# First group's up products of two quarters in float16, with w_in's bounds in two parts

## The chip, the cores and the metric

The kernel runs on one core of a Trainium2 chip. The time is device microseconds of one execution of the program. The engines are TensorE (PE; its weight loads are PEld), VectorE (DVE), ScalarE (ACT), GpSimd (POOL) and SyncE (SP, which issues nearly all DMAs). Each works off its own instruction list in order.

## The reference

Attention over a few memory slots, then a two-layer feed-forward block. Batch 8, 8 heads, 576 positions, head size 64, 32 slots:

```
a      = softmax(phi)                          # over the 32 slots
k_m, v_m = a^T k, a^T v                        # per head: 32 x 64
x      = softmax(q k_m^T / 8) v_m              # 4608 tokens x 512
h      = x w_in                                # 512 -> 2048
out    = max(0.01 h, h) w_out                  # 2048 -> 512
```

q, k, v and phi are float32. w_in and w_out are float64; the kernel reads their words and makes float32 of them itself.

## The kernel before

The kernel never forms x. It folds the attention's values into the weights: for batch b and quarter j of d_ff (512 of 2048 columns), v_m times w_in's quarter is a 256 x 512 matrix, and h is the attention weights times that matrix. Products of float32 accuracy are either float32 matmuls (four passes in the array, two records each in the trace) or three float16 passes: an operand is split into a float16 hi part and a float16 lo part (the rest), and hi x hi, lo x hi and hi x lo are added up. A split needs a power-of-two scale, which comes from a bound on the weights: squares are summed (ScalarE), transposed on TensorE, turned into a power of two on VectorE and spread to all partitions by a matmul.

Tokens are worked off in groups. Group 0 (384 tokens of batch 0) and group 1 (384 more) go by units of 256 of the 2048 columns; from then on groups of 256 tokens take another route, with one up and seven down products per quarter. Before the change, group 0 is wholly in float32, since the bounds of the weights are not known that early; group 1 and all later ones are in float16.

Every instruction's place is written by hand: two strings, OPENING and LATER, list the steps in order, and each engine gets its instructions in the order of that list. Steps that matter here:

- `i<j>.` and `o<j>.`: quarter j of w_in and w_out. `ld0` to `ld2` load three pieces (768, 768, 512 columns) into one of eight staging slots used in turn, so a load waits until the slot's last reader is done; `h`, `y`, `t` make float32 of a piece (h and y on ScalarE, h on VectorE for some pieces, t on VectorE); `b` sums the squares on ScalarE (L429). `k`, `l` and `s`, `m`, `n` make the float16 parts of the weights and of sums of their blocks.
- `ci.1` to `ci.4` and `co.1` to `co.4` (L489 to L512): the bounds of w_in and w_out, all four quarters at once: transpose, roots on VectorE, spreading matmul, factors on VectorE. `e.` (L1301, L1302): the scales of the folded weights of batches 0 and 1.
- `f0<j>.1` (L1242): the folded products of batch 0, quarter j, in float32 into two PSUM banks. `f0<j>.2` (L1614): ScalarE copies them to SBUF as float32.
- `u<u>.P<i>` (L1340): an up product of group 0, unit u (quarter u // 2), half i: two float32 matmuls of 384 columns. `u.V` (L1347): leaky relu on ScalarE. `u.O` (L1411): down products, three float32 matmuls of 512 columns.
- `W<b><j>.p` (L1242), `.h` (L1275, ScalarE), `.l` (L1281, VectorE): the folded weights of batch b, quarter j, and their float16 hi and lo parts for the halves g = 0, 1. For batch 0 these are made from the float32 copy in SBUF, for batch 1 from PSUM. `w1.1` is W10.p.
- `P<m>`, `V`, `C`, `L`, `O` (m = 8 to 15): the same units for group 1, in float16; C and L make hi and lo of the leaky result. `p`, `v`, `s`, `c`, `l`, `d`: the later groups.
- `a<b>.`: attention of batch b. Here: phi, kv, q (loads), A1 to A3, B0 (maximum of phi), B10, B20 (subtract, exp), C10 (slot sums, L794), D1, D2, D3 (their transposes and scale), E1 (scores, L1088), E2 (flips), S (softmax by chunks).
- `z.`: products of ones that keep TensorE busy at the start.

PSUM tiles named pa have three banks that are used in turn; folded products take two of them.

Of the kernel before, what the change touches and what calls it, by code (L numbers as in the profile page):

```python
# [77 lines left out]
C10 V11.1 W03.h0 a2.kv3 o0.l2 V11.0 o1.l0 W03.h1 o1.m2 o1.k1 O8.0 W12.l1 O8.1 O9.0 o2.k0 C11 P13.0
P12.1 L10 o3.s3 W03.l0 O9.1 o1.l2 o1.n2 o1.m3 i1.l1 o1.l1 a2.B20 L11 O10.0 W03.l1 W13.h0 V12.1 o2.l0
P13.1 o2.k2 o2.s0 V13.0 W13.l0 P12.0 a2.kv1 W13.h1 a2.C10 a2.B3 W13.l1 a1.S17 V13.1 C13 a2.C2 o1.n3  # L80
o2.m0 O10.1 V12.0 i1.l2 C12 o2.s1 O11.0 i2.k0 a2.C30 o2.k1 L12 P14.0 a2.C31 L13 o2.n0 P14.1 O11.1
o2.l1 a2.q0 o2.s2 o2.m1 o2.n1 V14.0 a2.C3k a2.C4 a2.D10 a1.S18 i2.l0 P15.0 V14.1 P15.1 a2.D3 a2.Q0
o2.m2 o2.s3 V15.0 o2.l2 a3.phi C14 O12.0 V15.1 p0.0 o2.m3 o3.k0 v0.0 o3.k2 O12.1 i2.k1 p0.1 o3.s0
C15 p0.2 L14 O13.0 i3.k1 o3.s1 v0.2 a2.q1 a3.A1 a2.Q1 v0.1 L15 a2.E1 p1.0 i2.l1 o3.s2 o3.l0 a2.E21
a2.E22 o3.k1 p0.3 o3.m0 O13.1 v0.3 o3.l1 v1.0 o2.n2 a2.E20 p1.1 c0.0 o2.n3 i2.k2 a3.A2 a2.D2 o3.l2
a2.D11 o3.n0 p1.2 v1.2 O14.0 v1.1 s0 a2.E3 a2.D4 o3.m3 p1.3 a3.A4 o3.m2 a2.E23 c0.1 O14.1 a2.D5 v1.3
O15.0 l0.0 p2.1 o3.m1 a2.S01 O15.1 c1.0 a2.S02 v2.1 o3.n1 a2.S03 Z1.0 l0.1 o3.n3 p2.0 Z1.2 a2.D6
v2.0 a3.A3 o3.n2 d0.0 d0.1 p2.2 d0.5 a3.kv s1 l1.0 p2.3 a2.S04 Z1.1 c1.1 d0.6 d1.1 d1.0 a3.B10 v2.3
# [1646 lines left out]
```

## Time and profile before

| | before |
|---|---|
| three runs | 648.1, 645.9, 647.3 us, median 647.3 us |
| profiled execution's own time | 647.43 us |
| its span, first to last instruction | 645.6 us |
| busy: TensorE, VectorE, ScalarE, GpSimd | 630.3, 529.7, 402.9, 14.3 us |
| share of the span | 98%, 82%, 62%, 2% |
| granted clock of TensorE | 1.00 over the span |
| read from HBM, written | 50.59 MB, 9.45 MB |

The time of the execution is 1.8 us longer than the span. A busy share is an average over stages. Rows of the trace give a line of the kernel (L1340 is line 1340), an engine, an operation and its tiles (output <- inputs); a number in brackets at the end is the time that the engine stood idle just before, and what released it. Matmuls are pipelined: a row's length holds the latency of the last one, so the cost of a matmul in a packed stretch is the distance from one start to the next.

### The profile page before, as it was taken

The page shows a single profiled execution, that of the slowest core. Times are in us where ns is not written, and L with a number is a line of the kernel's source. Part 1 is how long each engine was busy: PE and PEld are TensorE (multiplying, and loading weights), DVE is VectorE, ACT ScalarE, POOL GpSimd, SP SyncE. Part 2 cuts the span into 40 slices and gives each one's busy share as a digit, 9 for nine tenths or more (in the row PEclk, how much of TensorE's full clock was granted, in tenths as well). Part 3 has the DMA queues.
Part 4 walks back from the last instruction along what each step waited for, and adds up shares of the span by engine and source line. Part 5 has one row for each costly group of instructions (what it writes and reads, how often), then busy time and mean ns, then how long its engine had stood idle before and what let it go on. Part 6 is the DMA issues. An engine that isn't in the chain of part 4 may idle for free.

```text
span 645.6 us, 17428 instructions
## 1 busy us (share of the span) xinstructions
PE 630.3 (98%) x7437; PEld 496.7 (77%) x7437; DVE 529.7 (82%) x841; ACT 402.9 (62%) x699; POOL 14.3 (2%) x34
## 2 busy tenths in 40 slices
...
GB/s 318 363 372 274 304 46 4 120 106 13 172 99 42 186 50 83 133 71 78 39 188 22 13 2 101 79 144 46 2 92 19 6 29 33 4 29 6 34 17 50
DMA packets 85404, 61.16 MB, mean 95 GB/s; under 512 B 61648, under 2 KB 68560, under 8 KB 85328
## 3 DMA queue, kind: packets, MB, share of 16 engines
...
q8 instruction: 58, 0.95, 0.6%
q10 hardware_dynamic: 576, 0.56, 0.3%
q14 instruction: 18, 0.15, 0.1%
HBM read 50.59 MB, written 9.45 MB: 93 GB/s over the span
## 4 chain that ended last, share of the span: by engine, by line
PE 52%; DVE 6%; SPq 3%; issue 1%; ACT 1%; DMA 0%; DVEq 0%; ACTq 0%
PE po L1521 27%; PE ph L1453 17%; PE ph L1521 4%; SPq L621 3%; PE pa L1242 2%; DVE arena L1498 1%; DVE arena L986 1%; PE pa L794 1%; DVE r1k L656 1%; PE pa L1044 1%; DVE arena L1488 1%; SPq L1394 0%; DMA arena<-in_q_dram 0%; DVE arena L1489 0%; DVE t L1120 0%
## 5 line engine op out<-in xcount | busy, mean ns | idle before, releaser
L1521 PEld LDWEIGHTS <-arena 128*128 128x128 f16 x2520 | 242.0, 98 | 38.2 <-issue 8.5
L1453 PE MATMUL ph<-a,w_mem 128*128 128x256 f16 (+3 forms) x1656 | 157.0, 243 | 1.0 <-ACT wi L1472 0.7
L1521 PE MATMUL po<-wo,arena 128*128 128x256 f16 x1080 | 139.6, 273 | 1.0 <-DVE arena L1498 0.6
L1521 PE MATMUL po<-arena 128*128 128x256 f16 x1080 | 140.0, 273 | 0.0
L1453 PEld LDWEIGHTS <-w_mem 128*128 128x128 f16 x1656 | 128.6, 98 | 14.8 <-issue 4.6
L1474 ACT ACTIVATE wi<-ph,g_scs 128x256 f32<-128x256 f32 x112 | 53.0, 473 | 82.7 <-PE ph L1453 72.9
L1472 ACT ACTIVATE wi<-ph,g_scs 128x256 f32<-128x256 f32 x112 | 52.9, 472 | 66.1 <-PE ph L1453 64.1
L1498 DVE TENSOR_TENSOR arena<-arena 128x1024 f16<-128x1024 f32 (+1 forms) x58 | 69.9, 1205 | 28.2 <-ACT arena L1494 28.2
L1411 PE MATMUL po<-wo,arena 128*128 128x512 f16 (+1 forms) x240 | 77.1, 467 | 0.8 <-DVE wo L424 0.8
L1494 ACT CAST arena<-arena 128x1024 f16<-128x1024 f32 (+1 forms) x58 | 60.2, 1037 | 21.8 <-DVE arena L1490 17.7
L1498 DVE TENSOR_TENSOR arena<-wi,arena 128x768 f16<-128x768 f32 x56 | 52.9, 948 | 6.0 <-ACT arena L1494 5.9
L1521 PE MATMUL ph<-wo,arena 128*128 128x256 f16 x360 | 48.8, 273 | 0.4 <-DVE arena L1498 0.4
L1494 ACT CAST arena<-wi 128x768 f16<-128x768 f32 x56 | 46.6, 831 | 3.4 <-PE po L1521 2.9
L1488 DVE TENSOR_TENSOR arena<-wi 128x512 f32<-128x512 f32 x56 | 38.5, 687 | 8.5 <-ACT wi L1472 4.3
L1340 PE MATMUL ph<-a,w_mem 128*128 128x192 f16 (+1 forms) x232 | 38.0, 313 | 0.0
L1411 PEld LDWEIGHTS po<-wo,arena 128*128 128x128 f32 x96 | 17.4, 190 | 20.2 <-issue 18.4
L1281 DVE SCALAR_TENSOR_TENSOR w_mem<-pa,w_mem 128x512 f16<-128x512 f32 x40 | 26.9, 681 | 7.0 <-ACT w_mem L1275 7.0
L1242 PE MATMUL pa<-wi,vT 64*32 64x512 f16 (+1 forms) x704 | 29.5, 420 | 0.7 <-DVE w_mem L1281 0.7
L1275 ACT ACTIVATE w_mem<-pa 128x512 f16<-128x512 f32 x40 | 23.1, 598 | 8.1 <-PE pa L1242 2.9
L1490 DVE TENSOR_TENSOR arena<-wi,arena 128x256 f32<-128x256 f32 x56 | 23.8, 425 | 2.0
L1453 PE MATMUL ph<-a,arena 128*128 128x256 f16 (+3 forms) x216 | 24.9, 237 | 0.5 <-ACT wi L1472 0.5
L1489 DVE TENSOR_TENSOR arena<-wi,arena 128x256 f32<-128x256 f32 x56 | 23.8, 425 | 1.9
...
## 6 DMA issues: line engine op xcount, KB each, us to landing
...
```

What stands on the lines that cost most here:

```text
L1242: nc.tensor.matmul(pf[g][cols, :], lhs, rhs, start=(n == 0), stop=(n == len(passes) - 1), tile_position=(g * D, hh * M),)
L1281: nc.vector.scalar_tensor_tensor(tiles(t[:, 1]), w(g), ws, tiles(t[:, 0]), ALU.mult, ALU.subtract)
L1340: nc.tensor.matmul(ph[:, t0:t0 + n], lhs, rhs, start=(m == 0), stop=(m == len(seq) - 1))
L1411: nc.tensor.matmul(po, lhs, rhs, start=(f == 0 and m == 0), stop=(f == NQ * NF - 1 and m == len(seq) - 1),)
L1453: nc.tensor.matmul(ph[:, t0:t0 + n], lhs, rhs, start=(m == 0), stop=(m == len(seq) - 1))
L1472: nc.scalar.activation(dst, ph, AF.Prelu, scale=g_sc2n[:, j:j + 1], alpha=1.0 / SLOPE)
L1474: nc.scalar.activation(dst, ph, AF.Prelu, scale=g_sc2[:, j:j + 1], alpha=SLOPE)
L1488: nc.vector.tensor_tensor(gt[:, 0:2], two, gf[:, 1:3], ALU.subtract)
L1489: nc.vector.tensor_tensor(gt[:, 2], gf[:, 1], gt[:, 1], ALU.subtract)
L1494: nc.scalar.copy(dst[:, 0], src)
L1498: nc.vector.tensor_tensor(dst[:, 1], src, dst[:, 0], ALU.subtract)
L1521: nc.tensor.matmul(acc, g[:, x, s, u], rhs, start=(h == 0 and j == 0 and u == 0 and m == 0), stop=(j == NQ - 1 and u == 1 and m == 2), ski ...
```

## The change

Group 0's up products of quarters 2 and 3 (units u4 to u7) use the float16 parts W02 and W03, in three passes, where quarters 0 and 1 stay in float32. For that:

- The attention weights of group 0 get float16 parts as well: `a0.H0` (a cast on ScalarE) and `a0.H1` (a subtraction on VectorE), 128 x 768 each.
- f02.2 and f03.2, the float32 copies, are gone; W02's and W03's hi and lo parts are made from the products in PSUM, before the units that use them.
- w_in's bounds go in two parts, quarters 0 to 2 (`ci0.1` to `ci0.4`) and quarter 3 (`ci3.1` to `ci3.4`), each through transpose, roots, matmul and factors. The factors also make batch 0's fold scale and `h_sc`, the scale that the leaky step of u4 to u7 applies. `e.` makes batch 1's alone.
- Some buffers are assigned otherwise (`w_turn`, the place of a sum's temporary, and two buffers of the first later group).
- The order is the same for the first 110 steps, up to u1.P0, and another one behind it, in OPENING and in LATER.

```
@@ OPENING, from the 110th step on
-i1.y0 i1.t0 u0.P1 u1.V0 a0.S11 o0.h0 o0.y0 o0.h1 o1.ld1 i1.h2 i2.ld1 a0.S12 o1.ld2 o0.t0 o0.y1 o0.t1
...
-i2.ld0 o1.y0 u1.O1 u2.V1 o2.h0 a0.S14 a0.D4 u2.V0 i2.ld2 i2.h0 o1.t0 o2.ld1 i2.y0 u3.P0 u3.P1 i2.h2
-o1.t2 i2.t0 a1.phi i2.y2 i2.t2 o2.y0 o2.y1 f02.1 o2.ld2 u2.O0 o2.t0 o2.h1 f02.2 u3.V0 a1.A1 o2.h2
-a1.A2 a1.A3 a0.S15 i1.b o2.t1 a1.kv1 u4.P1 a1.B0 a1.kv0 o2.y2 a1.kv2 u3.O0 u3.V1 a1.kv3 u4.P0 a1.q1
-a1.B10 a0.S16 a1.B20 a1.q0 o0.b o2.t2 u4.V0 o1.b o2.b a1.B3 a1.C10 i3.ld1 a1.Q0 a1.C2 a1.C30 u5.P0
-a1.C31 u2.O1 a1.C4 i3.ld0 a1.Q1 i3.ld2 i3.h1 a1.C3k o3.ld2 a1.D11 i2.b a1.D5 a1.D10 a1.D2 u3.O1
-a1.D4 i3.y1 u4.V1 i3.t1 a1.D3 a1.E1 u5.V0 i3.y0 i3.h0 i3.y2 i3.t0 u4.O0 i3.h2 o3.y2 i3.t2 a1.E22
-u5.P1 a1.E20 i3.b a1.S01 a1.E21 a1.S02 f03.1 ci.1 u5.O0 a2.phi o3.h2 a1.S11 a0.S17 o3.ld1 o3.t2
-u5.V1 o3.y1 a1.S03 ci.2 a2.kv2 a1.S12 a0.S18 o3.h1 u4.O1 a2.A1 a1.S04 a1.S13 o3.t1 ci.3 f03.2 a2.A2
-ci.4 o3.ld0 e. w1.1 o3.h0 o3.y0 W00.h0 a1.S05 a1.S06 o3.t0 u6.P0 u7.P0 a1.S14 W10.h0 u6.V0 o0.s0
-W00.h1 a2.A4 o3.b u7.V0 u6.O0 W00.l0 o0.s1 W00.l1 co.1 a1.S07 W01.h0 a2.A3 a2.B10 co.2 u7.P1 W10.h1
-u6.P1 a2.kv0 co.3 a1.S08 i0.k1
+o0.h1 i1.y0 o0.h0 o0.y0 o0.y1 i1.t0 u1.V0 u1.P1 o1.ld1 o0.t0 u1.V1 o0.t1 i1.h1 a0.D2 i1.h2 i2.ld1
...
+o1.t2 i2.t0 a1.phi o2.h0 i2.t2 i2.b o2.t0 o2.ld2 u1.O1 u3.P1 u2.O0 u3.V0 ci0.1 a1.A1 a0.H0 u3.V1
+a1.A2 a1.kv1 o2.y1 ci0.2 o2.y2 u2.P1 a1.A3 a1.kv0 a0.H1 a1.kv2 ci0.3 a1.kv3 ci0.4 o2.h1 a1.B0 f02.1
+a1.B10 o2.h2 W02.h0 a1.B20 a1.q1 u3.O0 o0.b a0.S16 W02.h1 W02.l0 o2.t1 a1.B3 a1.q0 a1.C10 W02.l1
+W00.h1 i3.ld1 a0.S17 a1.C2 o2.t2 a1.C30 u4.P1 a1.C31 a1.Q1 u2.V1 u4.V1 u2.O1 i3.ld0 W00.h0 a1.C3k
+a1.C4 a1.D10 u5.P0 a1.D2 a1.Q0 o1.b a1.D3 W00.l0 i3.y1 i3.h1 a1.D4 u4.P0 u4.V0 a1.E1 W01.h0 i3.ld2
+i3.t1 i3.h0 o3.ld2 W00.l1 u5.V0 u3.O1 i3.y0 i3.y2 i3.h2 a2.phi o3.ld1 o3.ld0 u4.O0 W01.l0 a1.E22
+i3.t0 a1.E20 i3.t2 a1.S01 u5.P1 a1.D11 a1.E21 a0.S18 o2.b a1.S11 a1.S02 i3.b ci3.1 a1.D5 o3.h2 u5.O0
+a2.A1 ci3.2 ci3.3 o3.y2 o3.y1 o3.h1 a1.S03 a2.A2 f03.1 o3.h0 a1.S12 ci3.4 W03.h0 a1.S04 W03.h1
+W03.l0 a1.S05 o3.y0 W03.l1 e. u4.O1 o3.t1 u5.V1 o3.t0 o3.t2 o0.s0 a1.S13 u6.P0 w1.1 u6.V0 W01.h1
+a1.S14 o3.b a2.A4 u7.P0 o0.s1 a2.A3 u6.O0 W10.h1 u7.V0 a1.S06 co.1 co.2 u7.P1 W10.h0 a1.S07 W10.l0
+u6.P1 i0.k1 i0.k0 u7.V1
...
+    NJ0 = 2
...
-    w_turn = iter([4, 5, 0, 1, 4, 2, 0, 3] + [4, 0, 6, 1, 2, 3] * B)
+    w_turn = iter([4, 5, 0, 1, 2, 4, 3, 0] + [2, 3, 6, 1, 4, 0] * B)
...
-    def bounds(kind, steps):
-        cols = slice(0, NQ) if kind == "i" else slice(NQ, 2 * NQ)
+    def bounds(kind, steps, j0=0, j1=NQ):
+        n, x = j1 - j0, 0 if kind == "i" else NQ
+        cols = slice(x + j0, x + j1)
...
             nc.vector.tensor_scalar_mul(sw[:, cols], sw[:, cols], scale)
+            if kind == "i":
+                fold_scale(0, cols)
+                nc.vector.tensor_scalar(
+                    h_sc[:, cols], pw[:, cols], states[0]["pv"], A_SCALE**-2, ALU.mult, ALU.mult
+                )
...
         def w(g):
-            return tiles(w32[j][g]) if b == 0 else by_tile(src["w"][g])
+            if b == 0:
+                return tiles(w32[j][g]) if j < NJ0 else by_tile(first["f", j][g])
+            return by_tile(src["w"][g])
...
-            if G == 0:
+            if G == 0 and f < NJ0 * NF:
                 a0 = a_f32(b)[:, tbs].rearrange("p i (g x) -> p i g x", g=NG)
                 seq = [(w32[f // NF][g][:, fs], a0[:, :, g]) for g in range(NG)]
             else:
+                if G == 0:
+                    a = a_old
                 seq = [
                     (halves(w16(b, f // NF), g)[:, x, fs], a[:, tbs, y, g, cs])
                     for g in range(NG) for x, y in ((0, 0), (1, 0), (0, 1))
...
+    def halves_old(i):
+        of = a_f32(0)[:, 0:2].rearrange("p tb (g x) -> p tb g x", g=NG)
+        if i == 0:
+            nc.scalar.copy(a_old[:, :, 0], of)
+        else:
+            nc.vector.tensor_tensor(a_old[:, :, 1], of, a_old[:, :, 0], ALU.subtract)
+
     def leaky(dst, ph, G, u):
-        sc = H_SCALE0 if G == 0 else g_sc[:, u // 2:u // 2 + 1]
+        j = u // 2
+        sc = g_sc[:, j:j + 1] if G else h_sc[:, j:j + 1] if j >= NJ0 else H_SCALE0
         nc.scalar.activation(dst, ph, AF.Prelu, scale=sc, alpha=SLOPE)
...
-    for kind in "io":
-        bounds(kind, steps)
-    steps["e."] = fold_scales
+    bounds("i", steps, 0, NJ0 + 1)
+    bounds("i", steps, NJ0 + 1, NQ)
+    bounds("o", steps)
+    steps["e."] = lambda: fold_scale(1, slice(0, NQ))
```

## Rows read from the trace of the kernel before

**Rows 1.** Busy us by engine in three stretches (start:end, length, each engine with its instructions, granted clock, DMA share, GB/s).
```profile
28.50:83.60 55.10, 53.48 (x429) 25.26 (x427) 41.58 (x70) 49.52 (x77) 6.78 (x8) 1.00 0.88 303
83.60:240.00 156.40, 154.17 (x1924) 110.86 (x1917) 153.41 (x240) 111.96 (x190) 5.89 (x8) 1.00 0.34 85
240.00:265.00 25.00, 23.41 (x321) 19.36 (x318) 24.04 (x46) 14.25 (x27) 0.10 (x1) 1.00 0.36 73
265.00:600.00 335.00, 333.60 (x4118) 290.75 (x4117) 268.04 (x409) 192.54 (x346) 0.10 (x1) 1.00 0.22 54
```

**Rows 2.** TensorE in order of time (start us, length us, line, tiles, count).
```profile
58.79 2.39 PE L794 MATMUL pa<-arena 64*32 64x128 f32 x144
...
70.00 1.28 PE L1088 MATMUL pa<-arena,kT 32*32 32x192 f32 x63 [0.74 <-ACT kT L937]
...
76.94 0.27 PE L489 MATMUL pa<-ident,sq 128*4 128x128 f32 x1
77.05 5.31 PE L1411 MATMUL po<-wo,arena 128*128 128x512 f32 x12
82.29 0.38 PE L507 MATMUL pa<-diag,ones 4*128 4x4 f32 x2
82.60 1.09 PE L1242 MATMUL pa<-wi,vT 64*32 64x512 f32 x16
83.62 2.85 PE L1340 MATMUL ph<-a,w_mem 128*128 128x384 f32 x8
86.30 2.74 PE L1411 MATMUL po<-wo,arena 128*128 128x512 f32 x6
...
92.81 0.38 PE L507 MATMUL pa<-diag,ones 4*128 4x4 f32 x2 [1.08 <-DVE diag L501]
...
107.21 1.16 PE L1340 MATMUL ph<-a,w_mem 128*128 128x192 f16 x12
108.21 0.62 PE L1411 MATMUL po<-wo,arena 128*128 128x512 f32 x1
```

**Rows 3.** VectorE in order of time, around the steps ci.2 and ci.4 with e.
```profile
77.25 0.28 DVE L494 TENSOR_REDUCE m<-pa 4x1 f32<-4x128 f32 x1 [0.18 <-PE pa L489]
...
78.34 2.21 DVE L656 TENSOR_REDUCE r1k<-arena 128x128 f32<-128x1152 f32 x1
...
82.76 0.15 DVE L510 COPY pw<-pa 128x4 f32<-128x4 f32 x1
...
83.77 0.57 DVE L1173 STREAM_TRANSPOSE t<-t 128x384 f32<-128x384 f32 x1
```

**Rows 4.** VectorE's groups of instructions, 20 to 260 us (count, busy us, mean ns, idle before).
```profile
L1363 DVE TENSOR_TENSOR arena<-arena 128x768 f16<-128x768 f32 x8 | 7.6, 945 | 0.0
L1281 DVE SCALAR_TENSOR_TENSOR w_mem<-w_mem,ws 128x512 f16<-128x512 f32 x8 | 6.0, 745 | 0.0
L1281 DVE SCALAR_TENSOR_TENSOR w_mem<-pa,ws,w_mem 128x512 f16<-128x512 f32 x6 | 4.5, 742 | 0.0
```

**Rows 5.** ScalarE's groups of instructions, 20 to 260 us.
```profile
L1614 ACT COPY w_mem<-pa 128x512 f32<-128x512 f32 x8 | 4.3, 585 | 0.9 <-PE pa L1242 0.9
L1359 ACT CAST arena<-arena 128x768 f16<-128x768 f32 x8 | 6.7, 832 | 0.1
L1347 ACT ACTIVATE arena<-ph,g_scs 128x384 f32<-128x384 f32 x16 | 9.2, 581 | 3.1 <-PE ph L1340 2.9
L1347 ACT ACTIVATE arena<-ph 128x384 f32<-128x384 f32 x16 | 7.8, 488 | 0.3 <-PE ph L1340 0.3
L415 ACT ACTIVATE arena<-arena 128x768 f32<-128x768 f32 x14 | 12.9, 945 | 1.1 <-DMA arena<-in_moe_w_out_dram 0.9 <-DMA arena<-in_moe_w_in_dram 0.2
```

**Rows 6.** SyncE's DMA issues: the last quarter of w_in.
```profile
61.02 2.70 SPq L394 DMA_DIRECT2D arena<-in_moe_w_in_dram  x5
```

**Rows 7.** ScalarE in order of time: i3.h2 and i3.b.
```profile
72.05 0.67 ACT L404 ACTIVATE arena<-arena 128x512 uint32<-128x512 uint16 x1
...
73.47 1.91 ACT L429 ACTIVATE wi<-wi 128x2048 bf16<-128x2048 f32 x1
```

More of the change, by code (lines that the diff above doesn't have):

```diff
@@ L78 @@
[L78 to L88, printed above, removed]
@@ L180 @@
[L180 to L184 removed]
+W10.l1 co.3 u7.O0 co.4 o0.m0 i0.k2 W01.l1 a2.B10 a2.kv1 o0.m1 o0.k2 o0.k0 u6.V1 a2.B20 W11.p i0.l1
@@ new lines @@
+a2.D11 o2.n3 s0 O14.0 o3.n2 l0.0 c0.1 o3.n3 O14.1 p2.1 o3.m1 c1.0 O15.0 a2.D4 l0.1 a2.D5 v2.0 v2.1
+i3.k0 p2.3 a2.E23 s1 a2.S01 c1.1 v2.3 o3.n1 a2.S02 a3.A4 O15.1 p2.2 d0.0 i2.l1 p3.1 a2.S03 a3.kv
+Z1.2 Z1.1 Z1.0 d0.1 v2.2 d0.5 d0.6 a2.D6 i3.k2 l1.1 a3.A3 d1.5 l1.0 a3.B10 d0.2 c2.0 p3.0 v3.1
+a2.S04 d0.3 W20.p l2.0 s2 a3.B20 d1.0 d1.1 W20.h0 p3.3 i3.l0 i3.k1 d1.3 d0.4 v3.0 d1.4 a2.S05 d2.0
+p3.2 a2.S06 W20.l0 W20.h1 d1.2 a2.S07 v3.3 v3.2 a3.B3 W20.l1 a2.S08 a3.C10 a3.C2 d1.6 p4.1 p4.0
+i3.l1 c2.1 c3.0 l2.1 v4.1 v4.0 a3.C30 d2.6 a3.C31 a3.C3k d2.1 s3 l3.0 d2.2 c3.1 p4.2 a3.C4 d2.3 p4.3
@@ new lines @@
+v8.1 d5.4 a3.E20 v7.2 W30.p a3.E21 p8.3 p8.0 c7.0 W30.h1 d6.6 v8.0 l6.1 d6.1 d6.5 s7 v8.3 a3.S01
+p8.2 d6.0 W30.l1 d6.4 p9.1 a4.B20 l7.0 a4.B3 d7.0 W31.p d7.1 c7.1 v9.1 W30.h0 v8.2 l7.1 d6.3 W30.l0
+W31.h1 a3.S02 c8.0 W31.l1 x3.p p9.0 d6.2 d7.2 v9.0 p9.3 a3.S03 p9.2 s8 v9.2 a3.S04 l8.0 a4.C10 v9.3
+a4.q1 p10.0 p10.1 c8.1 d7.3 c9.0 x3.0 W31.h0 l8.1 d7.4 v10.0 a4.C2 s9 v10.1 x3.1 l9.0 d8.0 p10.2
+a3.S05 c9.1 p10.3 d7.6 v10.3 d9.0 x3.2 v10.2 a3.S06 d8.1 a4.q0 c10.0 p11.0 d8.3 d8.2 l9.1 p11.1 d7.5
@@ new lines @@
+a4.D11 x4.0 a4.D5 a4.D6 s13 d11.4 v14.1 d12.0 d11.3 x4.1 p14.2 c13.1 x4.2 p14.3 W33.l1 W40.p d12.5
+d13.0 a5.A4 v14.3 v14.2 l13.1 c14.0 x4.3 W40.h1 W40.h0 d12.6 d12.3 p15.0 p15.1 a4.S01 a5.A3 d13.3
+d12.4 s14 a5.B10 W40.l0 v15.0 v15.1 l14.0 d12.1 p15.2 p15.3 d13.4 d13.5 a4.S02 W40.l1 c14.1 d12.2
+v15.2 v15.3 a5.B20 p16.0 a4.S03 p16.1 v16.1 d13.1 v16.0 W41.p a5.B3 d13.6 l14.1 p16.3 z4.1 p16.2
+z4.0 W41.h1 c15.0 v16.3 v16.2 d14.4 d14.1 s15 l15.0 c15.1 d13.2 p17.1 p17.0 v17.1 d14.0 v17.0 d15.0
+l15.1 W41.l1 d14.3 a4.S04 p17.3 a5.C10 a4.S05 p17.2 d14.2 c16.0 d14.6 d15.2 v17.3 s16 l16.0 v17.2
@@ L185 @@
+z15.0 p59.2 d57.5 d56.2 d58.5 d57.2 v59.2 v59.3 c59.0 d58.0 d58.6 s59 l59.0 c59.1 d58.2 d59.0 d57.4
+d58.4 l59.1 end.p d59.2 d59.4 d59.3 d59.6 end.0 end.1 d59.5 d57.1 end.2 d58.1 d59.1 end.4 end.3
+end.5 end.z2 end.z1 end.z0
 """
```

239 lines of the change are left out of this document (117 added, 122 removed).

## Prediction

> **What bounds the kernel now.** I read the shares by engine first: TensorE is busy 98% of the span. A busy share is an average, so the busy time by stretch comes next [rows 1], because the change lies in one stretch. From 28.5 to 83.6 us (the opening from the change's first edited step to u6.P0) TensorE stands still 55.10 - 53.48 = 1.6 us, VectorE 13.5 us, ScalarE 5.6 us, and the DMA engines are 88% busy: TensorE is the bound, and the others wait for loads and for each other. From 83.6 to 240 us TensorE idles 2.2 us and VectorE 3.0 us of 156.4: both are full, and each TensorE gap there is short and ends, by the list of waits, mostly on VectorE. From 240 to 265 us TensorE idles 1.6 us, and the chain of waits runs through VectorE. So time is won by less TensorE work, if VectorE's operands come in time. Third came TensorE's instructions in order of time [rows 2]: from 57.4 us on they stand end to start, except for gaps of 0.74 us at 70.00, where a1.E1 waits for ScalarE, and of 1.08 us at 92.81, where the matmul of w_out's bounds waits for VectorE's diagonal.
>
> **TensorE work removed.** Two float32 up steps (8 records) run from 83.62 to 86.30: 1.34 us a step. A float16 step of group 1 (twelve matmuls of 192 columns, the same 6 x 384 columns as the new ones) takes 108.21 - 107.21 = 1.00 us [rows 2]. Eight steps (u4 to u7, two each) change: 8 x 0.34 = 2.72 us less. The float16 rate for six instructions of 384 columns is not in the trace; were the fixed part of an instruction halved with their number, they would come a little below 1.00, so 2.6 to 3.0 us is the range.
>
> **TensorE work added.** w_in's bounds go through the chip twice. The transpose takes 0.11 us (76.94 to 77.05) and the spreading matmul 0.31 us (82.29 to 82.60) [rows 2]: 0.42 us, and nothing if TensorE stands idle at that point anyway. If the matmul also waits for VectorE's diagonal as at 92.81, it costs 1.08 us more; in the new order u2.P1 (1.34 us) lies ahead of the first one and u5.O0 of the second, which hides VectorE's four instructions (77.25 to 78.34, 1.1 us [rows 3]). I take 0.42.
>
> **VectorE.** Added: a0.H1, a subtraction of 128x768 like L1363's, 0.95 us [rows 4]; the second roots, 1.1 us (77.25 to 78.34); the second factors, one more fold_scale and two h_sc instructions, about as much as the stretch 82.76 to 83.77, 1.0 us, which holds seven such instructions [rows 3]. In all 3.1 us more. Moved ahead of u6.P0: W00.l0, W00.l1, W01.l0 (0.745 each), all four lo parts of W02 and W03 (0.742 each) [rows 4]. Together the list of VectorE in front of u6.P0 grows by 2.2 + 3.0 + 3.1 = 8.3 us, against 13.5 us of idle time there [rows 1]. So after u6.P0 VectorE has some 5 us less to do than before, in the stretch where it is full.
>
> The lo parts of W02 and W03 now read PSUM, where L1281 read the float32 copy in SBUF: 742 ns against 745 [rows 4], no difference. The Trainium skill (Perfetto Trace Analysis, Optimizing Scalar/DVE Operations) gives a VectorE instruction about 65 ns more overhead on PSUM than on SBUF, by which the four would cost 0.26 us more, two of them in the chain of W03 below; the trace does not agree.
>
> **ScalarE.** Removed: four copies of f02.2 and f03.2, 4 x 0.585 = 2.34 us. Added: a0.H0, a cast of 128x768, 0.83; eight leaky steps whose scale is now a pointer, 581 against 488 ns, 0.74 [rows 5]. Net 0.8 us less; in front of u6.P0 it is 3 us more (W00.h1, W01.h0, W02.h and W03.h come ahead), against 5.6 us of idle time.
>
> **What is late next: u6.P0.** Before, u6.P0 needed f03.2 only. Now it needs W03's hi and lo parts, and these need w_in's last quarter loaded, converted, squared and bounded. TensorE itself would reach u6.P0 at 83.62 - 1.36 (four cheaper steps ahead of it) + 0.42 - 1.02 (w1.1's products, 82.60 to 83.62, are now behind it) = 81.7. The chain: i3.ld1 is issued at 61.02, when a1.C10 (58.79 to 61.1) gives its slot free [rows 2, 6]; i3.h2 ends at 72.7 (72.05 + 0.67); then the new order puts o2.b in front of i3.b, each 1.9 + 0.1 us, so i3.b ends at 76.7 instead of 75.5 [rows 7]. ScalarE then has seven steps in front of W03.h0 (a1.D5, o3.h2, o3.y2, o3.y1, o3.h1, a1.S03, o3.h0: 0.67 for a short conversion, 0.95 for a long one, less 0.1 of overlap each [rows 5, 7]), 4.3 us: 81.0. W03.h0 and h1 take 1.2 (0.6 each, as the copies of the same size from PSUM, L1614 [rows 5]), W03.l1 on VectorE 0.75: 83.0. TensorE waits 1.3 us there, and in this wait nothing is queued that could run, w1.1 being behind u6.P0. From below the wait is 0: a1.C10 can come 2.3 us earlier by its list (two up steps of 1.34 less ahead of it, one pass of w_in's bounds more), which frees the slots for w_in's last quarter earlier, if k and v have landed by then. From above it is 3.3 us, if the w_out pieces of o3 land 2 us late inside the ScalarE list. I take 1.3. a1.C10 itself now needs W02.l0, which frees the third PSUM bank: W02.l0 lies two short steps behind a1.B10 on VectorE, while TensorE does u3.O0 (2.6 us), so nothing is counted.
>
> **Stalls given back.** From 83.6 to 265 us TensorE idles 2.2 + 1.6 = 3.8 us, mostly for VectorE. With 5 us less of VectorE work behind u6.P0, between 0 and all of it goes. The 1.08 us at 92.81 should go, since fewer lo parts stand in front of the diagonal; of the other 2.7 I take a third: 1.9 us in all, for the TensorE saving itself makes VectorE later relative to it.
>
> **Sum.** -2.72 + 0.42 + 1.3 - 1.9 = -2.9 us on the profiled execution's own 647.43 us: 644.5 us. The shown median is 647.3, 0.1 us lower, which I leave out. Runs shown lie 2.2 us apart, so 0.3% (1.9 us) is about what can be told from no change; 644.5 is 0.4% below.
>
> **Rivals.** (a) The load of w_in's last quarter sets u6.P0. Then u6.P0 starts at 83.6 as now; what remains behind it is 1.36 us cheaper and 1.02 us (w1.1) longer, and no stall goes: 647.43 - 0.34 = 647.1, no change. For it: the DMA engines are 88% busy, and o2.b and four ScalarE conversions stand in the way. Against: 5.6 us of ScalarE idle time, and a slot that is free earlier.
>
> (b) Slower: VectorE is the bound from 83.6 to 240 us, and its added instructions push everything. It decides if VectorE cannot use its 13.5 us of idle time before 83.6, because it stands behind conversions that wait for loads. Then the moved lo parts only delay the conversions, u6.P0 starts at its old time or later, and the stretch grows by the added 3.1 us less the 0.3 us of (a): 650.2. For it: VectorE 98% full, in a list without choice. Against: TensorE's gaps there are only 2.2 us, and W00's, W01's and W02's lo parts wait for no load of the last quarter. The Trainium skill (Perfetto Trace Analysis, Identifying the Most-Contended Engine) judges TensorE by its weight loads, not by busy matmuls, and calls the engine of highest occupancy the one to work on; in that stretch weight loads fill 71% and VectorE 98% [rows 1], so the rule stands with this rival.
>
> (c) More than forecast: u6.P0 waits for nothing and all stalls up to 265 us go: -2.72 + 0.42 - 3.8 = -6.1, 641.3 us.
>
> **Chances.** Forecast (643 to 646) 0.52, (a) 0.26, (b) 0.13, (c) 0.09. The forecast's own range crosses -0.3% for a tenth of it, (a) reaches it for a tenth: faster 0.58, same 0.28, slower 0.14. The range is 641.8 to 648.3: it holds the forecast and (a) with the unknown waits at u6.P0 (0 to 3.3) and leaves out most of (b) and half of (c).
>
> **What would show it.** Right: eight up steps of twelve half-length, or six 384-column, float16 matmuls at 1.0 us each; VectorE idle below 6 us up to u6.P0; u6.P0 between 81.5 and 83.5 us; no gap at the matmul of w_out's bounds; TensorE's idle from there to 265 us near 2 us. Wrong: u6.P0 behind 84 us, TensorE gaps that end on W03's lo parts or on the group 1 halves, or the saving gone in new gaps behind 265 us, where the whole order is rewritten too and I count nothing (TensorE idles 335.0 - 333.6 = 1.4 us up to 600 us [rows 1], so little is to be won there and more can be lost).

## The result and the profile after

| | before | after |
|---|---|---|
| six runs each, on one chip | 645.90 to 649.67 us, median 647.69 | 638.67 to 641.28 us, median 640.36 |
| ratio | | 0.9883, 95% interval 0.9859 to 0.9906 |
| profiled execution's own time, span, granted clock | 647.43, 645.6 us, 1.000 | 638.67, 636.9 us, 0.999 |
| busy: TensorE, VectorE, ScalarE, GpSimd | 630.3, 529.7, 402.9, 14.3 us | 625.5, 532.7, 401.0, 14.1 us |

The forecast was 644.5 us: the sign was right, the gain is 7.3 us where 2.9 was forecast, and 640.36 lies below the range. In part of the executions TensorE's mean granted clock is 0.993 to 0.998 in place of 0.999 to 1.000, and these take some 2.4 us longer, so where a difference is small the medians of the two kinds are compared too, called full clock and lower clock from here on ("full" and "lower" in the table). The kernel before takes 646.6 us at full clock (56 executions over all comparisons) and 649.1 at the lower, the changed one 638.75 (4 executions) and 641.0.

The changed kernel's busy time by stretch (start:end, length, each engine with its instructions, granted clock, DMA share, GB/s), as [rows 1]:

```profile
28.50:83.60 55.10, 51.88 (x425) 25.18 (x424) 47.30 (x89) 51.69 (x80) 7.02 (x8) 1.00 0.85 291
83.60:240.00 156.40, 156.24 (x1978) 113.79 (x1977) 153.88 (x241) 112.36 (x189) 5.42 (x8) 1.00 0.36 91
240.00:265.00 25.00, 25.00 (x358) 21.47 (x356) 23.31 (x44) 13.83 (x27) 0.10 (x1) 1.00 0.53 152
265.00:600.00 335.00, 335.00 (x4121) 292.51 (x4120) 270.86 (x412) 193.20 (x350) 0.10 (x1) 1.00 0.20 48
```

TensorE idles 3.2 us up to 83.6 us, where it idled 1.6, and then 0.16 us up to 600, where it idled 5.2 (2.2 + 1.6 + 1.4). VectorE is as full as before from 83.6 to 240 (153.88 of 156.4 us, before 153.41).

TensorE of the changed kernel in order of time, as [rows 2]:

```profile
29.51 0.38 PE L365 MATMUL pa<-mdiag,ones 128*128 128x128 f32 x2
32.31 1.56 PE L1351 MATMUL ph<-a,w_mem 128*128 128x384 f32 x4 [2.42 <-ACT arena L1370]
...
59.36 2.16 PE L803 MATMUL pa<-arena 64*32 64x128 f32 x132 [0.69 <-DMA arena<-in_v_dram]
...
83.43 1.14 PE L1351 MATMUL ph<-arena,w_mem 128*128 128x384 f16 x6
...
89.19 2.11 PE L1351 MATMUL ph<-arena,w_mem 128*128 128x384 f16 x12
91.23 0.38 PE L511 MATMUL pa<-diag,ones 4*128 4x4 f32 x2
```

Two float16 steps take 91.23 - 89.19 = 2.04 us, 1.02 each. u6.P0 starts at 83.43 (before 83.62) without a wait, and the matmul of w_out's bounds (91.23) has none either. New are 2.42 us at 29.9, where u0.P1 waits for the leaky step u1.V0, which now stands behind five conversions on ScalarE, and 0.69 us in which a1.C10, which now comes earlier, waits for the load of v. The chain into u6.P0, i3.b on ScalarE and the two low parts of W03 on VectorE:

```profile
74.59 1.91 ACT L432 ACTIVATE wi<-wi 128x2048 bf16<-128x2048 f32 x1
```
```profile
81.63 1.41 DVE L1292 SCALAR_TENSOR_TENSOR w_mem<-pa,ws,w_mem 128x512 f16<-128x512 f32 x2
```

i3.b ends with its accumulator read at 76.6 us (forecast 76.7), W03.l1 at 83.04 (forecast 83.0).

**Where the 8.7 us of span went.** Three groups of TensorE's matmuls that both kernels hold in equal number, before and after (instructions | busy us, mean ns of one):

```profile
L1453 PE MATMUL ph<-a,w_mem 128*128 128x256 f16 (+3 forms) x1656 | 157.0, 243 | 1.0 <-ACT wi L1472 0.7 <-DVE w_mem L1281 0.3
L1521 PE MATMUL po<-arena 128*128 128x256 f16 x1080 | 140.0, 273 | 0.0
L1521 PE MATMUL po<-wo,arena 128*128 128x256 f16 x1080 | 139.6, 273 | 1.0 <-DVE arena L1498 0.6 <-DVE obs L1539 0.4
```
```profile
L1476 PE MATMUL ph<-a,w_mem 128*128 128x256 f16 (+3 forms) x1656 | 156.6, 243 | 0.0
L1544 PE MATMUL po<-wo,arena 128*128 128x256 f16 x1080 | 139.4, 273 | 0.0
L1544 PE MATMUL po<-arena 128*128 128x256 f16 x1080 | 138.4, 273 | 0.0
```

The same matmuls are "busy" 2.2 us less. A row's length holds a modelled end, so a wait shorter than that end does not show as idle time, it lengthens the busy time. The starts of the matmuls show it without modelled ends: both traces hold 3383 distances from a float16 matmul of 256 columns to the next start, 109 ns in the median, and they add up to 376.8 us before and 372.2 after. Of these 4.6 us only 3.4 stand in the trace of the kernel before as idle time; 1.2 are hidden waits.

The sum: work -8 x (1.34 - 1.02) + 0.42 = -2.1; TensorE's busy time fell by 4.8, so 2.7 us of hidden waits went in all, as the remainder (by the starts of all matmuls of the full array, from 28.5 us on, the hidden part falls from 8.9 to 6.3, 2.6 us); visible idle time +1.6 (28.5 to 83.6), -5.1 (83.6 to 600), -0.4 (ahead of 28.5 and the tail). Together -8.7.

Where it was won can be read by comparing the times at which the two kernels have the same matmuls left to do (each form at its median distance; good to about half a us, as the two lists differ in detail). The changed kernel leads by some 1.0 us at u6.P0, 1.7 at 160 us, 6.6 at 290 and 8.8 at the end. So the stretch right behind u6.P0, where VectorE's list holds fewer steps than before, brought little; most came from 160 to 290 us, and 2.2 us behind that.

### The profile page after: what moved, and what is told of

Same layout as the page of the kernel before. It is cut to its first block, busy times and chain, and to the rows that moved or that the text cites. A ratio compares the mean times of both kernels' runs of the same rounds, so it can differ in the third digit from the quotient of the medians.

```text
span 636.9 us, 17462 instructions
## 1 busy us (share of the span) xinstructions
PE 625.5 (98%) x7456; PEld 495.9 (78%) x7456; DVE 532.7 (84%) x853; ACT 401.0 (63%) x696; POOL 14.1 (2%) x34
## 4 chain that ended last, share of the span: by engine, by line
PE 84%; DVE 7%; DMA 4%; ACT 4%; issue 1%; SPq 1%; DVEq 0%; ACTq 0%
PE po L1544 37%; PE ph L1476 25%; PE ph L1544 6%; PE po L1434 6%; PE pa L1251 3%; PE pa L803 2%; ACT arena L418 1%; PE ph L1351 1%; DMA arena<-in_v_dram 1%; PE pa L1053 1%; DMA arena<-in_q_dram 1%; DMA wo<-in_k_dram 1%; DVE w_mem L1292 1%; DMA arena<-in_moe_w_in_dram 1%; ACT arena L407 1%
## 5 line engine op out<-in xcount | busy, mean ns | idle before, releaser
L1476 PEld LDWEIGHTS <-w_mem 128*128 128x128 f16 x1656 | 128.3, 98 | 14.6 <-issue 4.4
L1544 PE MATMUL po<-arena 128*128 128x256 f16 x1080 | 138.4, 273 | 0.0
L1351 PE MATMUL ph<-a,w_mem 128*128 128x192 f16 (+1 forms) x200 | 27.4, 286 | 2.6 <-ACT arena L1370 2.4
L1292 DVE SCALAR_TENSOR_TENSOR w_mem<-pa,w_mem 128x512 f16<-128x512 f32 x40 | 26.8, 679 | 3.4 <-ACT w_mem L1286 3.4
L1351 PEld LDWEIGHTS <-w_mem 128*128 128x128 f16 x216 | 18.6, 98 | 9.5 <-issue 5.1
```

The costliest lines, as they stand in the source:

```text
L1292: nc.vector.scalar_tensor_tensor(tiles(t[:, 1]), w(g), ws, tiles(t[:, 0]), ALU.mult, ALU.subtract)
L1351: nc.tensor.matmul(ph[:, t0:t0 + n], lhs, rhs, start=(m == 0), stop=(m == len(seq) - 1))
L1476: nc.tensor.matmul(ph[:, t0:t0 + n], lhs, rhs, start=(m == 0), stop=(m == len(seq) - 1))
L1544: nc.tensor.matmul(acc, g[:, x, s, u], rhs, start=(h == 0 and j == 0 and u == 0 and m == 0), stop=(j == NQ - 1 and u == 1 and m == 2), ski ...
```

## The experiments

Each was timed beside the kernel before on the same chip. The kernel before, at full clock, had medians of 646.2 to 646.6 us in these comparisons and 647.7 in that of new_order_p4_to_p14_only, no_l_in_group1_after and xv_on_scalare, so a difference of two medians is good to about 1 us, and some of them rest on one or two executions.

| run | median us | ratio to before, 95% interval | full | lower |
|---|---|---|---|---|
| changed kernel, first comparison | 640.36 | 0.9883, 0.9859 to 0.9906 | 638.8 | 640.9 |
| f32_in_new_order | 643.88 | 0.9939, 0.9913 to 0.9965 | 643.3 | 644.2 |
| f16_in_old_order | 647.89 | 0.9996, 0.9976 to 1.0015 | 646.5 | 648.1 |
| new_opening_old_rest | 646.58 | 0.9983, 0.9965 to 1.0001 | 645.8 | 646.7 |
| old_opening_new_rest | 648.18 | 0.9996, 0.9974 to 1.0019 | 646.6 | 648.4 |
| old_until_p4_new_rest | 642.52 | 0.9921, 0.9890 to 0.9951 | 642.4 | 644.3 |
| new_until_p4_old_rest | 646.00 | 0.9969, 0.9951 to 0.9987 | 645.1 | 646.0 |
| new_order_p4_to_p14_only | 646.97 | 0.9976, 0.9955 to 0.9997 | 645.5 | 647.9 |
| vectore_5us_more | 648.25 | 1.0004, 0.9986 to 1.0022 | 646.3 | 648.3 |
| vectore_8us_more_mid | 647.43 | 0.9991, 0.9974 to 1.0008 | 645.9 | 647.8 |
| vectore_8us_more_late | 640.61 | 0.9893, 0.9870 to 0.9916 | 638.9 | 641.0 |
| no_low_parts_in_before | 644.19 | 0.9963, 0.9948 to 0.9979 | 644.2 | none |
| no_l_in_group1_after | 639.40 | 0.9855, 0.9831 to 0.9878 | 638.4 | 640.3 |
| one_pass_less_in_group1_after | 640.73 | 0.9901, 0.9881 to 0.9922 | none | 640.7 |
| u1V0_earlier | 638.35 | 0.9860, 0.9834 to 0.9886 | 638.4 | none |
| sums_on_gpsimd | 641.11 | 0.9906, 0.9885 to 0.9927 | 641.1 | none |
| xv_on_scalare | 640.01 | 0.9867, 0.9844 to 0.9891 | 640.0 | 641.5 |
| u1V0_alone | 638.44 | 0.9865, 0.9842 to 0.9887 | 638.4 | none |
| after_same_chip | 640.78 | 0.9893, 0.9872 to 0.9913 | 638.7 | 641.1 |

**The two halves of the change, each alone.** Float32 up products in the new order, then float16 ones in the old order (there on a constant operand; group 0's output is meaningless in both):

```diff
 f32_in_new_order, up products of units u4 to u7
-    seq = [(halves(w16(b, f // NF), g)[:, x, fs], a[:, tbs, y, g, cs]) ...]
+    seq = [(w16(b, f // NF)[g][:, fs], a0[:, :, g]) for g in range(NG)]
 f16_in_old_order, the same place
+    seq = [(halves(w32[f // NF], g)[:, x, fs], a[:, tbs, y, g]) ... for x, y in ((0, 0), (1, 0), (0, 1))]
```

> The changed kernel with its order, buffers, bounds and waits, but the up products of u4 to u7 are two float32 instructions on the same buffers again (the words of the float16 parts read as float32, so group 0's output means nothing). Theory A, the order: the float16 products are worth only TensorE's own 8 x 0.34 = 2.7 us, the other 4.6 us of the gain are the new order's: 640.4 + 2.7 = 643.1 us, ratio to the kernel before 0.993, and TensorE's idle time behind u6.P0 stays near nothing. Theory B, the float16 products loosen the full stretch and so bring more than their own time: 645 us or above, with TensorE gaps of 2 us or more back between 84 and 265 us.

> The kernel before with its order, but the up products of u4 to u7 are six float16 instructions of 384 columns on a constant tile (so group 0's output means nothing). Theory A: at most TensorE's own saving, 647.7 - 2.7 = 645.0 us, and less where VectorE is late, as it is full behind 83.6 us: 645 to 647. Theory B: 643 us or below.

At full clock the order alone (with the other new steps, but float32 products) gives 646.6 - 643.3 = 3.3 us, float16 alone 0.1, both 7.9; the intervals of the two ratios lie apart. In the old order the float16 saving turns into a wait at the bounds of w_out, 3.23 us where 1.08 was [rows 2]; the profiled execution is one at the lower clock, which falls behind this wait (1.00 from 84 to 92 us, 0.57 from 92 to 100). TensorE, 84 to 100 us:

```profile
92.95 0.59 PE L507 MATMUL pa<-diag,ones 4*128 4x4 f32 x2 [3.23 <-DVE diag L501]
```

**The order cut at the end of the opening.**

```diff
 new_opening_old_rest: the changed kernel
 OPENING = new
-LATER = new
+LATER = the steps left, in the old order
 old_opening_new_rest: the kernel before
 OPENING = old
-LATER = old
+LATER = the steps left, in the new order (W02's and W03's parts ahead of W12's and W13's)
```

> The changed kernel with its new OPENING, but the steps of LATER in the order of the kernel before (those that are left). Theory A1, the new order behind the opening removed the stalls: the time is 645 to 646.5 us (only the 1.9 us by which the opening and the float16 products help), TensorE idles 3 us or more between 84 and 265 us. Theory A2, the opening did it, because VectorE has 5 us less to do behind u6.P0: 640 to 642.5 us, TensorE idle time there below 1.5 us.

> The kernel before with its OPENING and float32 products, but the steps of LATER in the changed kernel's order, W02's and W03's parts put in front of the first parts of W12 and W13. Theory A1: it gains what the order behind the opening is worth, 642.5 to 644 us. Theory A2: 646.5 to 648.5 us, since VectorE is as late as before.

Neither half gives anything that can be told from no change by its interval, against 7.3 us for the whole. With the new rest TensorE waits 6.1 us from 84 to 160 and then no more up to 300; with the old rest it waits 2.4 us from 160 to 265 and 1.5 from 300 to 500. It may be that a cut makes waits of its own, where one list needs early what the other had put off; so the cut was made again at 190 us, where the two lists nearly coincide.

```diff
 old_until_p4_new_rest: the kernel before
 ... d2.6 c2.1 l2.1 v4.1 a3.C30 p4.3
-p4.0 d2.3 s3 d2.4 a3.C3k ...
+p4.0 v4.0 a3.C31 a3.C3k s3 l3.0 d2.2 ...   (all steps left in the new order)
 new_until_p4_old_rest: the changed kernel, the other way round
 new_order_p4_to_p14_only: the first of the two, in the old order again from p14.0 on (at 266 us)
```

> The kernel before, its work and its list of steps unchanged up to the first product of the fifth late unit (p4.0, at about 190 us); from there on the steps that are left stand in the changed kernel's order. All float32 up products of the old opening stay, and VectorE gets none of its 5 us of relief. Order theory (the new order of the rest takes the waits away by itself, whatever was done before it): no visible wait of TensorE from 200 us on, where the kernel before has 0.05 + 1.59 + 0.53 + 0.87 = 3.0 us of them, and the short waits under modelled ends go as well: 642 to 644 us. Relief theory (the waits go because VectorE has 5 us less to do in 84 to 240 us): waits as before, 646.5 to 648 us.

> The changed kernel up to p4.0, float16 up products and all; from there on the old order. Order theory: the changed kernel's lead at that point (2.6 to 4.5 us between 178 and 235 us in the share of late columns done) is kept, and the old order's waits of 3 us behind it are back: 643.5 to 645.5 us. Relief theory: as the changed kernel, 640 to 641 us, since VectorE is relieved as there.

> The kernel before, its work unchanged; its list in the new order only from p4.0 (about 190 us) to p14.0 (about 285 us), in the old order ahead of it and behind it. With the new order kept to the end the time was 5.6 us below the kernel before. If the gain is made where VectorE is full (it binds up to about 265 us) and the work that is put off there is later done in VectorE's idle time: most of it stays, 643 to 644.5 us. If it is made behind 285 us: 646.5 to 648 us. If the old order makes up for what was put off: 646 to 648 us, with TensorE's waits back in 285 to 320 us.

The new list behind 190 us gives the kernel before 4.2 us at full clock (3.8 against the kernel before on its own chip, 5.6 by the medians), with all its float32 products and without any relief of VectorE ahead of it. The changed kernel up to there, with the old list behind it, keeps 1.5 (1.0 on its own chip). Kept only up to p14.0, the new list gives 1.1 (2.2 on its own chip). In the traces p14.0 comes at 266 us, where TensorE's instructions begin to differ from those of the first of the three, and not at 285 as written down. Nor does the result place the rest of the gain behind 266 us, since this cut is followed by waits: from 265 to 300 us TensorE stands idle 1.10 us, where the kernel before and the first of the three show none. Its busy time there, and the longer of the two waits:

```profile
265.00:300.00 35.00, 33.90 (x518) 29.35 (x516) 32.16 (x49) 21.55 (x39) 0.00 (x0) 1.00 0.31 97
```
```profile
276.36 0.83 PE L1521 MATMUL po<-arena 128*128 128x256 f16 x6 [0.82 <-DVE obs L1539]
```

By the matmuls left to do, the first of the three gains some 3.6 us on the kernel before from 190 to 290 us and 1.7 behind. What comes behind 265 us is what the forecast counted at nothing. The busy time of the first, 84 to 265 and 265 to 600 us:

```profile
84.00:265.00 181.00, 179.49 (x2278) 133.20 (x2277) 177.07 (x282) 127.48 (x219) 6.13 (x9) 1.00 0.38 97
265.00:600.00 335.00, 334.87 (x4128) 292.29 (x4127) 271.37 (x415) 194.03 (x351) 0.10 (x1) 1.00 0.21 49
```

VectorE is as full to 265 us as before (177.07 against 177.09 us of 181), and behind it does 3.3 us more (271.37 against 268.04 [rows 1]).

**VectorE made slower and faster.**

```diff
 vectore_5us_more: behind V8.0 to V12.1; ..._mid: behind v3.1 to v12.1; ..._late: behind v20.1 to v29.1
+nc.vector.tensor_reduce(scales[:, 14:16], <ones, 128x2x128>, AX.X, ALU.max)   # twice at each of ten steps
 no_low_parts_in_before: the kernel before (the high part stands in for the low one in group 1)
-W00.l0 W00.l1 ... W03.l1
 no_l_in_group1_after: the changed kernel (likewise)
-L8 ... L15
```

> The changed kernel with 20 added VectorE reductions (128x256, about 0.3 us each, some 5 to 6 us in all) spread behind the ten steps V8.0 to V12.1, between about 97 and 130 us; nothing reads them. Order theory (VectorE runs ahead of TensorE there, and the new order has the lead to take it): under 1.5 us longer, 640.5 to 642 us, waits of TensorE behind 100 us under 2 us. Relief theory (VectorE is the bound in 84 to 240 us, so what it gets more TensorE waits for): the whole 5 to 6 us, 645 to 646.5 us.

> The same 20 reductions behind v3.1 to v12.1, between about 180 and 260 us, where VectorE is busy 98% and TensorE has no visible idle time in the changed kernel. VectorE theory: one for one, 647 to 649 us. If TensorE's missing idle time means that VectorE no longer binds there: 640.5 to 643 us.

> The changed kernel with the same 20 VectorE reductions (8.3 us in the run before) behind the steps v20.1 to v29.1, between about 300 and 385 us, where VectorE is busy 84% of the time. VectorE theory: there TensorE is the bound and VectorE takes them in its idle time: under 1.5 us longer, 640 to 642 us. If VectorE's list binds to the end: 648 us.

> The kernel before, order unchanged, without the eight low parts of batch 0's folded weights (W00.l0 to W03.l1, 8 x 0.745 = 6.0 us of VectorE, all between 84 and 125 us); group 1's matmuls read the high part in their place, so TensorE does as many matmuls and group 1's output of batch 0 lacks the low part. It tests the step 'stalls given back' by itself: 6 us less VectorE work and nothing else. VectorE theory (from 84 to 265 us TensorE goes as fast as VectorE's list lets it, visible idle or not): 5 to 6 us less, 641.5 to 643 us. As forecast (TensorE's visible idle of 3.8 us is the ceiling and half of it goes): 645 to 646.5 us. Order theory: no change, 647 to 648.5 us.

> The changed kernel without the eight low parts of group 1's leaky results (L8 to L15, 8 x 1.04 = 8.3 us of VectorE between 90 and 150 us); the down products read the high part in their place, so TensorE does as many matmuls and group 1's output is meaningless. Mirror of the added 8.3 us, which cost 8. If VectorE alone sets the time of that stretch: 632 to 634 us. If TensorE is as full as VectorE there, so that only lateness counts: 638.5 to 640.5 us. In the kernel before, 6.0 us less VectorE work gave 3.1 us; by that share 636.

The added 20 reductions took 0.42 us each, 8.3 us, more than the 5 to 6 written down. At the lower clock (641.0 for the changed kernel) they cost 7.3 us at 100 to 130 us, 6.7 at 180 to 260, and nothing behind 300. So up to some 260 us what VectorE gets more, TensorE waits for, although in the changed kernel TensorE shows next to no idle time there (0.16 us). With the added work the waits can be seen: 5.9 us of idle time from 84 to 265 us in vectore_5us_more, 5.2 in vectore_8us_more_mid:

```profile
84.00:265.00 181.00, 175.11 (x2210) 128.21 (x2209) 177.51 (x292) 122.22 (x207) 6.65 (x10) 1.00 0.35 87
```
```profile
84.00:265.00 181.00, 175.81 (x2211) 127.93 (x2210) 177.62 (x291) 122.20 (x208) 6.04 (x10) 1.00 0.35 89
```

The reverse fails: 8.3 us less VectorE work between 90 and 150 us gave 0.3 us at full clock (0.8 at the lower). In the kernel before 6.0 us less gave 2.4 at full clock, about the share that the forecast gave back (1.9 for 5), not 5 to 6; by the medians it gave 3.1, as all twelve executions were at full clock there, and of the kernel before beside it 11 of 23 were not.

**TensorE made faster, in the changed kernel.**

```diff
 one_pass_less_in_group1_after
-    ... for x, y in ((0, 0), (0, 1), (1, 0))]
+    ... for x, y in ((0, 0), (0, 1))]
```

> The changed kernel with two of the three float16 passes in group 1's down products (48 matmuls of 512 columns less on TensorE, 0.216 us each, 10.4 us, between 95 and 150 us; group 1's output lacks the low part of the leaky result). VectorE's work is unchanged. If VectorE alone sets the time of that stretch: under 1.5 us less, 639 to 640.4 us. If TensorE alone does: 10 us less, 630 us. If both are full at once, neither is worth much alone: 2 to 4 us less, 636.5 to 638.5 us.

10.4 us of TensorE's work less gave 640.7 us, all at the lower clock, against 641.0 of the changed kernel's executions at the lower clock. The two are not quite alike, since the clock of this kernel's profile is 1.00 from 32 to 36 us and falls later (0.98 from 84 to 160 us). But against 638.75 at full clock it gave nothing either. That looks as if VectorE alone set the time; yet less VectorE work gave next to nothing too. From 84 to 265 us, this kernel, then no_l_in_group1_after:

```profile
84.00:265.00 181.00, 173.27 (x2261) 130.66 (x2260) 176.28 (x279) 124.82 (x215) 5.53 (x9) 0.99 0.38 99
```
```profile
84.00:265.00 181.00, 181.00 (x2308) 134.06 (x2307) 171.16 (x275) 126.77 (x217) 6.36 (x10) 1.00 0.38 99
```

With less TensorE work TensorE stands still 7.7 us and VectorE stays full; with less VectorE work it is the other way round. In the new list the two engines are level: each is the bound as soon as the other gets less.

**Versions that may beat both.**

```diff
 u1V0_alone (u1V0_earlier also moves w1.1 ahead of u6.P0)
-o0.h1 i1.y0 o0.h0 o0.y0 o0.y1 i1.t0 u1.V0 u1.P1
+o0.h1 i1.y0 u1.V0 o0.h0 o0.y0 o0.y1 i1.t0 u1.P1
 sums_on_gpsimd (on u1V0_earlier)
-nc.vector.tensor_tensor(tmp(x), y, z, op)
+nc.gpsimd.tensor_tensor(tmp(x), y, z, op)
 xv_on_scalare (on u1V0_earlier)
-nc.vector.tensor_scalar_mul(x_v[:, g], v_sums, r)
+nc.scalar.activation(x_v[:, g], v_sums, AF.Copy, scale=r)
```

> The changed kernel with two steps moved in the opening: the leaky step u1.V0 two conversions earlier on ScalarE (TensorE's wait of 2.42 us at 29.9 us is for it), and the fold product w1.1 (1.05 us) ahead of u6.P0. Order theory with fixed due times: the 2.4 us are won at 30 us; at u6.P0 the low part of the fourth quarter's weights, ready at 83.0 us, takes back what is over 1.4 us, and the chain of bounds takes more at co.3; 639 to 640.5 us, best guess 639.7. If whatever TensorE wins early is kept: 638 us. If the two conversions that are pushed back delay a down product: 640.5 to 642 us.

> The kernel of u1V0_earlier with the 16 block subtractions of w_out (L462, 128x512 float32, 0.68 us each on VectorE, 10.9 us in all, between 84 and 150 us) on GpSimd, which is idle there; a 128x384 subtraction took GpSimd 0.83 us, so about 1.1 us each. VectorE theory: TensorE gains until it is the bound itself; its waits left are those under the modelled ends: 2 to 5 us less, 633.5 to 636.5 us, best guess 635. If GpSimd's reads slow VectorE, or the high sums on ScalarE now wait for GpSimd: 638 to 641 us.

> The kernel of u1V0_earlier with the scaling of the slot values (L890, two 128x64 instructions of 0.28 us per batch, 14 in all, six of them between 84 and 265 us) on ScalarE in place of VectorE: 1.7 us off VectorE in the stretch where it binds, 2 us on ScalarE (0.31 us each), which is busy 65 to 75% there. VectorE theory: 0.8 to 1.7 us less than 638.35, 636.7 to 637.6 us. If ScalarE's place in the list makes it late: 638 to 639.5 us.

> The changed kernel with the leaky step u1.V0 four places earlier in the opening and nothing else. In five runs of kernels with the changed opening TensorE's wait of 2.1 to 2.6 us at 29.9 us was followed by a granted clock of 0.57 to 0.68 in 32 to 36 us, in two (the changed kernel's own profile among them) it was not. Clock theory (the median of the changed kernel holds some 1.7 us of that): wait under 1.1 us, clock 1.00 in 28 to 40 us, 638 to 639 us, spread under 2 us. If the lists alone count: 639.5 to 640.5 us.

> The changed kernel as it is, beside the kernel above on one chip, so that the two compare: 639.5 to 641 us. Clock theory: its profile shows a clock under 0.7 in 32 to 36 us and a span of 638.5 us, or 1.00 there and 636.9.

u1V0_alone ran in 638.14 to 638.60 us, on one chip with the changed kernel's 638.64 to 641.46. At full clock it is only 0.3 us better; but all ten runs of u1V0_alone and u1V0_earlier were at full clock, and eight of the changed kernel's twelve were not. The wait of 2.4 us at 29.9 us is behind that: of all kernels here with the changed opening, 64 of 84 executions with that wait were at the lower clock, and 1 of 22 without it. It is not the only such place, as 48 of 104 executions of the kernel before, which lacks the wait, were at the lower clock too. The changed kernel's opening in vectore_8us_more_mid, then u1V0_alone:

```profile
32.34 2.93 PE L1351 MATMUL ph<-a,w_mem 128*128 128x384 f32 x4 [2.41 <-ACT arena L1370]
```
```profile
29.94 1.56 PE L1351 MATMUL ph<-a,w_mem 128*128 128x384 f32 x4
32.50 3.70 PE L1434 MATMUL po<-wo,arena 128*128 128x512 f32 x8 [1.00 <-DVE wo L427]
```

Four matmuls that take 1.56 us take 2.93 behind the wait, and the granted clock of 32 to 36 us is 0.57: partly at 1.2 in place of 2.4 GHz. In the changed kernel's own profile the same wait of 2.42 us is followed by 1.56 us at clock 1.00. It falls in some executions and not in others.

xv_on_scalare came out 1.6 us above its base. Its profile shows a step made late by ScalarE's list: ScalarE stands at the moved step (L890) for 1.79 us until VectorE has made its factor, the leaky step comes behind it, and TensorE waits 1.88 us for that, a wait that the base lacks. (This execution is one at the lower clock; the clock falls behind the wait, to 0.57 from 64 to 68 us.)

```profile
62.98 0.52 ACT L890 ACTIVATE x_v<-pa,r 128x64 f32<-128x64 f32 x2 [1.79 <-DVE r L837]
```
```profile
63.94 4.54 PE L1434 MATMUL po<-wo,arena 128*128 128x512 f32 x6 [1.88 <-ACT arena L1370]
```

sums_on_gpsimd lost 2.8 us. VectorE's rows from 84 to 265 us in u1V0_earlier, then in sums_on_gpsimd, and GpSimd's there:

```profile
L468 DVE SCALAR_TENSOR_TENSOR arena<-arena,sw 128x512 f16<-128x512 f32 x12 | 8.8, 743 | 0.0
L1292 DVE SCALAR_TENSOR_TENSOR w_mem<-pa,w_mem 128x512 f16<-128x512 f32 x13 | 8.6, 676 | 0.0
L1386 DVE TENSOR_TENSOR arena<-arena 128x768 f16<-128x768 f32 x8 | 8.2, 1040 | 0.0
```
```profile
L468 DVE SCALAR_TENSOR_TENSOR arena<-arena,sw 128x512 f16<-128x512 f32 x12 | 12.3, 1031 | 0.4 <-ACT arena L465 0.2
L1386 DVE TENSOR_TENSOR arena<-arena 128x768 f16<-128x768 f32 x8 | 10.7, 1349 | 0.0
L1292 DVE SCALAR_TENSOR_TENSOR w_mem<-pa,w_mem 128x512 f16<-128x512 f32 x12 | 7.9, 673 | 0.0
```
```profile
L462 POOL TENSOR_TENSOR arena<-wo 128x512 f32<-128x512 f32 x6 | 10.4, 1735 | 17.6 <-ACT arena L1382 6.8 <-ACT arena L465 4.7 <-DVE arena L468 4.2
```

GpSimd took 1.74 us for one in this group, not 1.1, and VectorE's subtractions with two SBUF operands grew from 743 to 1031 and from 1040 to 1349 ns in the mean. Taken one by one they fall in two kinds. Of L468's twelve, seven ran beside no GpSimd subtraction and took 742 ns, five ran beside one and took 1435; of L1386's eight, four took 945 and four 1753. The Trainium skill (SBUF — State Buffer, Who interferes with whom) says that a VectorE instruction with two SBUF inputs contends with a GpSimd instruction that reads SBUF. These rows agree with it. L1292, with one operand in PSUM, stayed at 673 ns, but none of the twelve ran beside a GpSimd subtraction, so whether it would contend is not shown. Over the whole span VectorE was busy 534.0 us, in the base 533.2: all that was moved off it came back. What the 2.8 us of loss are made of is not shown.

## Why the prediction was wrong

- **TensorE work removed and added: right.** 1.02 us a step where 1.00 was taken, and 0.42 us for the second pass: -2.1 us, forecast -2.3.
- **What is late next, u6.P0: the chain right, the place of the wait wrong.** The chain ended at 83.04 (forecast 83.0). TensorE did not reach u6.P0 at 81.7 but at 83.43, since it had lost 2.42 us at 29.9 and 0.69 at 58.7 to steps that the new list had put late; I had not followed ScalarE's list at u1.V0. The price is about the same: 1.6 us more idle time in the opening, forecast 1.3.
- **VectorE: its relief was half of what I took.** It had done 47.30 - 41.58 = 5.7 us more by 83.6 us, and 3.0 of these are new work (532.7 - 529.7; forecast 3.1). So 2.7 us of relief, not 5, and 7.8 us of idle time up to there, where below 6 was to show the forecast right. I had counted the list in front of u6.P0 as worked off. When u6.P0 started, VectorE still had 2.8 us of that list to do (three conversions of o3 and o0.s0), in the kernel before 1.5 [rows 3]. Still, most of what was put in front went into what had been its idle time, which is where rival (b) fails. VectorE around u6.P0, in the kernel before and in the changed one:

```profile
84.27 0.92 DVE L424 SCALAR_TENSOR_TENSOR wo<-arena 128x768 uint32<-128x768 uint32 x1
```
```profile
83.28 2.44 DVE L427 SCALAR_TENSOR_TENSOR wo<-arena 128x768 uint32<-128x768 uint32 x3
85.64 0.68 DVE L462 TENSOR_TENSOR arena<-wo 128x512 f32<-128x512 f32 x1
```

- **Stalls given back: the step that failed.** I let go "1.9 us in all" of the 3.8 us that TensorE visibly idles up to 265, and "count nothing" behind. Gone are 5.1 us of visible waits up to 600 us (3.6 of them up to 265) and, as the remainder of the busy time, 2.7 of hidden ones: 7.8. There were two errors in the one step. First, visible idle time was taken for the ceiling, where a wait shorter than a matmul's modelled end shows as busy time. Second, the waits were tied to how much VectorE has to do, and not to the order in which it does it. The runs say the reverse: relief in the old order is worth what I took (2.4 us for 6.0), but the new list takes waits away without any relief (4.2 us from 190 us on). And the saving on TensorE, 2.6 us of its work, is worth about nothing in the old list and 3.2 (lower clock) to 4.6 us (full clock) in the new one; TensorE idles 1.26 us from 84 to 160 us there with float32 products, 0.16 with float16 ones.
- **Rival (c)**, all stalls to 265 us gone, was the nearest, and its condition came true. Its price, 641.3 us for the profiled execution, fell 2.6 short of the 638.67 measured, by the same two errors.
- **Rival (b)** had a true premise. More work on VectorE from 84 to 260 us does make the kernel longer, as the 7 us for 8.3 added show; but ahead of u6.P0 its list had the room for the added 3.1. The Trainium skill (Perfetto Trace Analysis, Identifying the Most-Contended Engine) would have the engine of highest occupancy improved first. Here that is VectorE, 98% full from 83.6 to 240 us, against weight loads that fill 73% (113.79 of 156.4 us). The added work agrees with the rule, but taking 8.3 us from VectorE gave 0.3, and here the measurement decides: two engines were level.

What stays open: which of the list's moves make the gain. Cut at 190 us the new list works; cut at the opening's end it does not, and behind a cut at 266 us waits follow. Of single moves only u1.V0 was tried, one that the new list had made worse.
